# Cast and output buffer counts, the engine that zeroes small operands, and the order of steps in a fused retention and token-mixing kernel

## The chip, the cores and the metric

The kernel runs on one core of a Trainium2 chip. The metric is device time in microseconds (us); 103.92 us is the median of three runs of the kernel before (103.59 to 105.15).

A run is called slow when it is more than 1.5% above the fastest run of the same kernel. A ratio is the mean time of one kernel's fast runs over that of the other's fast runs of the same rounds, so it is not quite the ratio of the medians quoted beside it. Names of engines: PE is the matrix engine, DVE vector, ACT scalar, POOL GpSimd, SP the engine that issues all transfers.

## The reference, cut to what matters

```python
# q, k, v: (B=4, H=8, S=768, D=64) float32
for t in range(S):                               # retention, per head
    state = gamma * state + outer(k[t], v[t])
    y[t]  = q[t] @ state / sqrt(D)
x     = y as (4, 768, 512)
W_tok = scale * (x @ w_q) @ (x @ w_k).T          # token mixing, per batch
out   = relu(W_tok @ x) @ w_out                  # (4, 768, 512) float32
```

## The kernel before

The work is cut into 12 pairs of chunks, three pairs to a batch. Each engine's instructions follow one list of steps, `ORDER`, which an annealer found. A step names the operation, the pair and sometimes the half, then the engine (`:A`, `:V`, `:P` for ACT, DVE, POOL) and the PSUM banks (`@`). The steps that the argument uses:

- `ck`, `cq`, `cv`: cast of k, q, v to bf16 (k and q with the decay factors), into one of `N_CAST` buffers;
- `trk`, `trq`, `xt`: eight transposes on PE; `ekT`, `eqT`, `exN` copy their result out of PSUM;
- `st`: adds k times v to the running state in PSUM; `es` copies the state to SBUF;
- `mx`: mixing matmul, `r` its relu, `pj` the output projection, `eo` copies it to an output buffer and issues the store;
- `warmup`, `fill`: matmuls on zeros that compute nothing; they were put in to keep PE busy, in the hope of a higher granted clock.

```python
N_CAST, ... , N_OUT = 4, ... , 6
...
bank7_ps = psum.tile([128, 512], FP32, name="bank7_ps")
fill_ps  = bank7_ps[:, 256:512]          # the fills write here
state_ps = bank7_ps[:, 0:256]...         # the running state lives here
...
for part in LOADS:                       # k0 q0 v0 k1 q1 k2 q2 v1 v2 W K1 WO Q1 V1
    ... nc.sync.dma_start(...)           # every load and store: SP, one queue
...
def cast(e, name, p, table):
    t = buf(name + "s", p % N_CAST, [2, H, D], BF16)
    ...
    elif casts[name, b] == NP and b + 2 < B:
        load(name, b + 2)                # loads of batches 2 and 3, after the casts of b
...
def fill(e, at, n):
    for _ in range(n):
        nc.tensor.matmul(out=fill_ps, lhsT=warm[:, 0:128], rhs=warm[:, 0:256],
                         start=False, stop=False, skip_group_check=True)
...
def es(e, at, p, c):                     # evicts the state of bank 7
    ... DVE: one tensor_tensor with a mask; ACT: two copies ...
...
def eo(e, at, p, j):
    o = buf(f"o{j}_", p % N_OUT, [DM], FP32)
    copy(e, o, st["o_ps", j])
    nc.sync.dma_start(out=dst[:, j], in_=o)
```

In the program as built, a copy into a used output buffer waits until the store of its previous content has landed (7.25 us in e4, 8.14 in e9).

## Time and profile before

| | before |
|---|---|
| time, median | 103.92 us |
| span of the profile | 103.6 us |
| PE / DVE / ACT / POOL busy | 87% / 64% / 57% / 57% |
| moved, at a mean of | 26.69 MB, 258 GB/s |
| first mixing matmul | 32.07 us |
| last load issued / first store issued / first store landed | 58.76 / 61.84 / 71.1 us |
| last copy of an output | 99.69 us |

Read it as three parts. Until 32 us (the head) PE depends on casts, copies and loads and is partly idle. From there to about 75 us PE is nearly full while the transfers still stream. After that PE sets the pace and the remaining stores go out. A loss in the middle or the end is taken to come out at the end directly, since PE has little slack there: it is busy for 38.45 of 41.06 us from 32.07 to 73.13 us, and for 26.31 of 26.56 us from there to 99.69. The lines themselves stand in the prediction.

### The profile page before, as it was taken

What the parts mean: (1) busy time and instruction counts of PE and PEld (TensorE: products, weight loads), DVE (VectorE), ACT (ScalarE), POOL (GpSimd) and SP (SyncE); (2) the same over time, 40 slices, a digit from 0 to 9 for tenths busy, and PEclk for the clock granted to TensorE, in tenths of its full rate; (3) what the DMA queues carried; (4) which work ended last, traced back from release to release, by engine and by line L of the source; (5) the groups of instructions that cost most, each with busy time, mean ns of one, the idle gap of its engine ahead of it and who ended that gap; (6) DMA issues with size and microseconds to landing.
All of it is one profiled execution on the core that took longest, in us unless ns stands there. A gap on an engine that the chain in (4) does not pass through costs nothing.

```text
span 103.6 us, 3459 instructions
## 1 busy us (share of the span) xinstructions
PE 90.2 (87%) x1477; PEld 61.3 (59%) x1485; DVE 66.6 (64%) x90; ACT 59.5 (57%) x106; POOL 58.7 (57%) x73
## 2 busy tenths in 40 slices
PE   5997876875996999897998999999999999999940
PEld 2345554664884645565895575889666589533410
DVE  3043699754534636989587885796996875625630
ACT  6004508642735665564779777787489796655420
POOL 6999914807953999096699997599930000000000
PEclk9999999999589999999999999999999999999999
DMA  0999998998999999598989999979954220046572
GB/s 23 314 347 346 348 350 220 304 303 321 358 331 301 297 252 334 135 334 278 328 243 308 276 345 357 340 247 364 398 213 164 101 101 6 0 158 247 202 296 112
DMA packets 26079, 26.69 MB, mean 258 GB/s; under 512 B 1744, under 2 KB 20176, under 8 KB 26064
## 3 DMA queue, kind: packets, MB, share of 16 engines
q1 hardware_dynamic: 26064, 26.48, 79.1%
q8 instruction: 11, 0.18, 0.7%
q14 instruction: 4, 0.03, 0.1%
HBM read 20.19 MB, written 6.29 MB: 255 GB/s over the span
## 4 chain that ended last, share of the span: by engine, by line
PE 66%; DVE 13%; POOL 8%; ACT 6%; issue 3%; DVEq 0%; POOLq 0%; ACTq 0%
PE bank_ps L704 17%; PE bank_ps L394 9%; DVE at L462 6%; PE bank_ps L600 5%; PE duo_ps L439 4%; DVE at L455 3%; PE bank_ps L551 3%; PE bank_ps L683 3%; PE bank_ps L624 3%; PE bank_ps L657 3%; PE duo_ps L704 3%; POOL ks L356 2%; PE bank_ps L506 2%; PE bank_ps L634 2%; PE bank_ps L535 2%
## 5 line engine op out<-in xcount | busy, mean ns | idle before, releaser
L462 DVE TENSOR_TENSOR at<-duo_ps,cmask 128x1024 bf16<-128x1024 f32 x18 | 21.4, 1216 | 2.2 <-PE duo_ps L439 2.2
L362 POOL TENSOR_TENSOR ks<-k_st,fk 128x512 bf16<-128x512 f32 x18 | 18.8, 1076 | 5.5 <-PE bank_ps L551 5.5
L704 PE MATMUL bank_ps<-wout_sb,relu 128*128 128x512 bf16 x78 | 19.7, 380 | 0.4 <-issue 0.2
L362 POOL TENSOR_TENSOR qs<-q_st,fq 128x512 bf16<-128x512 f32 x16 | 16.3, 1050 | 6.2 <-DMA q_st<-in_q_dram 6.2
L704 PEld LDWEIGHTS <-relu 128*128 128x128 bf16 x96 | 8.5, 98 | 9.0 <-issue 0.8
L156 ACT COPY o<-bank_ps 128x512 f32<-128x512 f32 x15 | 8.7, 590 | 7.3 <-PE bank_ps L704 7.3
L158 POOL CAST vs<-v_st 128x1024 bf16<-128x1024 f32 x10 | 10.5, 1073 | 4.2 <-DMA v_st<-in_v_dram 4.1
L156 ACT CAST s_sb<-bank_ps 128x256 bf16<-128x256 f32 (+1 forms) x20 | 7.4, 372 | 6.6 <-PE bank_ps L551 4.5
L156 ACT COPY qT<-bank_ps 128x1024 bf16<-128x1024 bf16 x7 | 7.1, 1015 | 5.4 <-PE bank_ps L394 5.4
L696 ACT ACTIVATE relu<-bank_ps 128x512 bf16<-128x512 f32 x15 | 8.5, 599 | 2.5 <-PE bank_ps L683 2.5
L156 ACT CAST xT<-bank_ps 128x512 bf16<-128x512 f32 x12 | 7.0, 590 | 3.6 <-PE bank_ps L524 1.4
L455 DVE TENSOR_TENSOR at<-duo_ps,cmask 128x1024 bf16<-128x1024 f32 x6 | 7.3, 1220 | 2.2 <-PE duo_ps L428 1.6
L329 PE MATMUL bank_ps<-warm 128*128 128x512 bf16 x24 | 7.3, 477 | 1.2 <-DVE warm L227 1.2
L394 PE MATMUL bank_ps<-identity,qs 128*128 128x128 bf16 x88 | 6.8, 220 | 1.4 <-DVE kT L158 0.7
L551 PE MATMUL bank_ps<-vs,ks 128*64 128x64 bf16 (+1 forms) x200 | 6.8, 197 | 1.0 <-ACT s_sb L156 0.9
L394 PEld LDWEIGHTS <-qs 128*128 128x128 bf16 x96 | 5.8, 98 | 3.1 <-issue 1.1
L158 DVE COPY x<-bank_ps 128x1024 bf16<-128x1024 bf16 x7 | 4.8, 688 | 4.3 <-PE bank_ps L600 4.3
L439 PE MATMUL duo_ps<-qT,kT 64*128 64x128 bf16 x144 | 6.6, 217 | 0.9 <-DVE qT L158 0.5
L394 PEld LDWEIGHTS <-ks 128*128 128x128 bf16 x96 | 5.7, 97 | 2.4 <-issue 0.9
L600 PE MATMUL bank_ps<-identity,xT 128*128 128x128 bf16 x88 | 6.7, 225 | 0.0
L551 PEld LDWEIGHTS <-ks 128*64 128x64 bf16 (+1 forms) x200 | 5.0, 110 | 2.8 <-issue 1.1
L158 DVE CAST xT<-bank_ps 128x512 bf16<-128x512 f32 x7 | 4.7, 688 | 2.9 <-PE bank_ps L524 1.3
(96 smaller groups left out, 166.0 us busy)
## 6 DMA issues: line engine op xcount, KB each, us to landing
out_dram<-o SPq DMA_DIRECT2D x24, 256.0 KB, 2.5
k_st<-in_k_dram SPq DMA_DIRECT2D x3, 512.0 KB, 6.0
q_st<-in_q_dram SPq DMA_DIRECT2D x3, 512.0 KB, 6.0
v_st<-in_v_dram SPq DMA_DIRECT2D x3, 512.0 KB, 6.2
wout_stage<-in_moe_w_out_dram SPq DMA_DIRECT2D x1, 1024.0 KB, 10.9
wq_stage<-in_moe_w_q_dram SPq DMA_DIRECT2D x1, 128.0 KB, 6.4
wk_stage<-in_moe_w_k_dram SPq DMA_DIRECT2D x1, 128.0 KB, 5.2
k_st<-in_k_dram SPq DMA_DIRECT2D x3, 0.2 KB, 12.2
```

What stands on the lines that cost most here:

```text
L156: nc.scalar.copy(out=out, in_=in_)
L158: ENGINES[e].tensor_copy(out=out, in_=in_)
L329: nc.tensor.matmul(out=bank(6), lhsT=warm[:, 0:128], rhs=warm, start=True, stop=True)
L362: ENGINES[e].tensor_tensor(out=t[:, j].rearrange("p (o m) d -> p o m d", o=2), in0=in_[:, j].rearrange("p (m o) d -> p o m d", o=2), in1=t ...
L394: nc.tensor.transpose(ps[:, i, hp, :] if whole(name, p // NP) else slots[:, :, hp, i, :], pairs[p][name + "s"][:, i, 2 * hp : 2 * hp + 2, ...
L439: nc.tensor.matmul(out=ps[:, x, m, :], lhsT=st["kT"][rows(x), i, m, :], rhs=st["qT"][rows(x), i, m, :], start=(m == 0), stop=(m == HP - 1) ...
L455: nc.vector.tensor_tensor(out=t.rearrange("p x (hi j) t -> p (x hi) (j t)", j=2), in0=ps.rearrange("p x (hi j) t -> p (x hi) (j t)", j=2), ...
L462: nc.vector.tensor_tensor(out=t.rearrange("p x hp t -> p (x hp) t"), in0=ps.rearrange("p x hp t -> p (x hp) t"), in1=cmask.rearrange("p o ...
L551: nc.tensor.matmul(out=state_ps[rows(x), m, :], lhsT=st["ks"][ps, slot, 2 * m + x, :], rhs=st["vs"][ps, slot, head(p, m, x), :], start=(n ...
L600: nc.tensor.transpose(ps[:, c, a, :], xT(p, a, c), identity)
L696: nc.scalar.activation(out=dst, in_=st["mx"][half], func=ACT.Relu)
L704: nc.tensor.matmul(out=ps, lhsT=st["relu", a // 2][:, a % 2, j], rhs=wout_sb[:, a, :], start=(a == 0), stop=(a == NDM - 1),)
```

## The change

Four edits: six cast buffers instead of four for each of q, k and v; four output buffers for each half instead of six, which pays for them in memory; the zeroing of the small operands on vector instead of GpSimd, which was late with its first cast; and a newly annealed order, with 28 warm-ups instead of 24 and 41 fills instead of 5. The order's diff replaces the whole list.

```diff
-warmup.24 cv.0:A cq.0:V trq.0@4 ck.0:P trk.0@5 eqT.0:V fill.1
+warmup.28 ck.0:V trk.0@4 ekT.0:A cq.0:V fill.6 trq.0@5 eqT.0:V
+fill.6 sc.0.0@0+1 cv.0:P eat.0.0:V sc.0.1@2+3 st.0.0 es.0.0:A fill.6
+st.0.1 ck.1:P in.0.1@4 ia.0.0@5 eat.0.1:V ia.0.1 trk.1@6 ex.0.0:V
+ck.2:V es.0.1:V ex.0.1:A ekT.1:A cq.1:P fill.3 trq.1@4 xt.0@5
 ... (cut)
-pj.5.1@4 ... pj.5.0@2 ... eo.5.1:A eo.5.0:A          (pair 5 fifth)
+r.5.1:A r.5.0:A pj.4.1@4 eo.4.1:A trq.8@2 eat.7.1:V in.7.0@5+6 in.7.1
+ia.7.0 st.7.1 xt.6@4 eqT.8:A ...                      (pair 4, half 1, fifth)
 ... (cut)
-N_CAST, ..., N_OUT = 4, 3, 6, 4, 3, 6, 8, 2, 6
+N_CAST, ..., N_OUT = 6, 3, 6, 4, 3, 6, 8, 2, 4
 ...
-        nc.gpsimd.memset(t, 0.0)          # four state buffers; dmask likewise
+        nc.vector.memset(t, 0.0)
```

More of the change, by code (lines that the diff above doesn't have):

```diff
@@ L18 @@
 ORDER = """
-warmup.24 cv.0:A cq.0:V trq.0@4 ck.0:P trk.0@5 eqT.0:V fill.1
-st.0.0 ekT.0:V fill.1 sc.0.0@0+1 eat.0.0:V es.0.0:A st.0.1 es.0.1:A
-ck.1:P in.0.1@4 sc.0.1@2+3 eat.0.1:V trk.1@5 ekT.1:V ck.2:V cq.1:P
-ia.0.0@6 fill.2 trq.1@5 ia.0.1 eqT.1:A trk.2@2 in.1.0@5 sc.1.1@0+1
-ex.0.1:A cv.1:P ekT.2:A ex.0.0:V cq.2:V trq.2@4 eat.1.1:V sc.1.0@2+3
-st.1.0 eat.1.0:V cv.2:P W:P eqT.2:A sc.2.1@0+1 xt.0@4 es.1.0:A
-in.1.1@6 ia.1.0 ia.1.1 st.1.1 es.1.1:V exN.0:V wqk.0@2 ex.1.1:A
-eat.2.1:V ex.1.0:A in.2.0@4 st.2.0 es.2.0:A sc.2.0@0+1 eat.2.0:V xt.1@5
@@ L27 @@
-exN.1:A ew.0:A in.2.1@6 ia.2.0 ia.2.1 wqk.1@5 ex.2.1:V ex.2.0:A
-wqk.2@4 xt.2@6 exN.2:V ew.2:A ew.1:A fill.1 za.0@4 zm.0
-ez.0:A mx.0@4+5 r.0.1:A ck.3:P ck.4:P ck.5:P cq.3:P cq.4:P
-cq.5:P cv.3:P cv.4:P cv.5:P WO:V mx.1@6+2 r.0.0:A r.1.1:A
-trk.3@5 trk.4@4 ekT.3:A ekT.4:V pj.0.0@2 trk.5@4 r.1.0:A pj.0.1@5
-eo.0.1:A eo.0.0:V ekT.5:V mx.2@6+2 pj.1.1@4 r.2.0:V pj.1.0@5 eo.1.1:A
-trq.3@4 r.2.1:A pj.2.1@6 eo.2.1:A eqT.3:V eo.1.0:A sc.3.0@0+1 eat.3.0:V
-trq.4@4 sc.3.1@2+3 pj.2.0@5 eat.3.1:V eqT.4:A sc.4.0@0+1 eat.4.0:V eo.2.0:A
@@ L35 @@
-sc.4.1@2+3 trq.5@4 st.3.0 es.3.0:V ia.3.0@5+6 ia.3.1 in.3.1 st.3.1
-eqT.5:A eat.4.1:V es.3.1:A sc.5.1@0+1 st.4.0 es.4.0:V ex.3.1:A sc.5.0@2+3
-eat.5.1:V eat.5.0:V in.4.0@4+6 ia.4.0 in.4.1 ia.4.1 st.4.1 es.4.1:A
-st.5.0 ex.4.1:V ex.4.0:A ex.3.0:V es.5.0:A in.5.0@4+2 ia.5.1 in.5.1
-ia.5.0 ex.5.0:A ex.5.1:A xt.4@6 exN.4:V xt.3@5 wqk.3@4 exN.3:A
-ew.3:A xt.5@6 wqk.4@2 wqk.5@4 ew.4:A ck.7:P ck.6:P trk.6@5
-trk.7@2 exN.5:V cq.6:V ew.5:A zm.1@4 ekT.6:A trq.6@6 ekT.7:A
-ez.1:V mx.3@4+5 r.3.1:A cq.7:P eqT.6:V sc.6.0@0+1 eat.6.0:V r.3.0:A
@@ L43 @@
-sc.6.1@2+3 trq.7@5 pj.3.1@4 eqT.7:A pj.3.0@6 eo.3.1:A mx.5@4+5 sc.7.0@0+1
-ck.8:P eat.6.1:V eo.3.0:A r.5.1:A trk.8@2 cv.6:P st.6.0 ia.6.0@6+5
-ia.6.1 eat.7.0:V sc.7.1@0+1 r.5.0:A es.6.0:A in.6.1 st.6.1 cq.8:P
-pj.5.1@4 ex.6.1:A es.6.1:A ex.6.0:A ekT.8:V trq.8@5 pj.5.0@2 eat.7.1:V
-cv.7:P cv.8:P eqT.8:V mx.4@5+6 sc.8.1@0+1 st.7.0 eo.5.1:A eo.5.0:A
-in.7.0@4+2 ia.7.0 es.7.0:A ia.7.1 r.4.1:A r.4.0:V st.7.1 es.7.1:A
-eat.8.1:V wqk.6@5 in.7.1 sc.8.0@0+1 st.8.0 ew.6:A ck.9:P xt.6@5
-trk.9@6 es.8.0:A ex.7.0:V ex.7.1:V wqk.7@4 exN.6:A in.8.0@2+5 in.8.1
@@ L51 @@
-eat.8.0:V ia.8.1 ia.8.0 ekT.9:A ck.10:P cq.9:P ew.7:V trk.10@4
-xt.7@6 ex.8.1:V ex.8.0:A xt.8@5 trq.9@2 ekT.10:A exN.7:V eqT.9:V
-exN.8:V wqk.8@4 ew.8:A sc.9.1@0+1 eat.9.1:V sc.9.0@2+3 cq.10:P trq.10@6
-eat.9.0:V pj.4.0@4 pj.4.1@5 eqT.10:A sc.10.0@0+1 eo.4.0:V cv.9:A eo.4.1:A
-zm.2@6 st.9.0 ez.2:A es.9.0:A ia.9.0@4+2 ia.9.1 mx.6@5+6 eat.10.0:V
-in.9.1 r.6.0:A st.9.1 sc.10.1@0+1 r.6.1:V cq.11:P ck.11:P cv.10:P
-cv.11:P trq.11@5 trk.11@6 ex.9.1:V es.9.1:A ex.9.0:A pj.6.0@4 ekT.11:V
-eqT.11:A pj.6.1@5 eat.10.1:V st.10.0 eo.6.0:A sc.11.1@2+3 eo.6.1:A sc.11.0@0+1
@@ L59 @@
-mx.7@4+6 es.10.0:A wqk.9@5 st.10.1 r.7.0:A eat.11.1:V r.7.1:A es.10.1:A
-in.10.0@4+2 in.10.1 ia.10.0 ia.10.1 st.11.0 ew.9:A eat.11.0:V in.11.0@5+6
-ia.11.1 ia.11.0 es.11.0:V in.11.1 ex.11.1:V ex.10.0:A ex.10.1:A xt.9@4
-xt.10@2 ex.11.0:A xt.11@5 exN.11:V exN.10:V exN.9:A wqk.11@6 ew.11:V
-wqk.10@4 ew.10:A pj.7.1@5 eo.7.1:A mx.8@4+6 za.3@2 zm.3 r.8.1:V
-r.8.0:A pj.7.0@5 ez.3:A pj.8.1@4 mx.9@6+2 eo.7.0:A eo.8.1:V pj.8.0@5
-r.9.1:A r.9.0:A mx.10@4+2 eo.8.0:A r.10.0:V pj.9.0@6 eo.9.0:V pj.9.1@4
-eo.9.1:V r.10.1:A mx.11@5+6 pj.10.0@2 eo.10.0:V pj.10.1@4 eo.10.1:V r.11.0:A
@@ L67 @@
-r.11.1:A pj.11.1@5 eo.11.1:V pj.11.0@6 eo.11.0:A
+warmup.28 ck.0:V trk.0@4 ekT.0:A cq.0:V fill.6 trq.0@5 eqT.0:V
+fill.6 sc.0.0@0+1 cv.0:P eat.0.0:V sc.0.1@2+3 st.0.0 es.0.0:A fill.6
+st.0.1 ck.1:P in.0.1@4 ia.0.0@5 eat.0.1:V ia.0.1 trk.1@6 ex.0.0:V
+ck.2:V es.0.1:V ex.0.1:A ekT.1:A cq.1:P fill.3 trq.1@4 xt.0@5
+eqT.1:A trk.2@6 sc.1.0@0+1 cq.2:V fill.5 trq.2@4 sc.1.1@2+3 exN.0:A
+eat.1.0:V ekT.2:A eqT.2:A cv.1:P fill.3 st.1.0 sc.2.0@0+1 eat.1.1:V
+cv.2:P es.1.0:A ck.5:P ck.4:P fill.1 sc.2.1@2+3 st.1.1 in.1.1@4
@@ new lines @@
+es.1.1:V fill.2 st.2.0 eat.2.1:V W:A wqk.0@5 ck.3:P es.2.0:A
+ew.0:A in.1.0@6 in.2.1@2 eat.2.0:V cq.4:P in.2.0@5 ia.2.0 ia.2.1
+ex.2.0:V ex.2.1:A fill.4 xt.2@5 exN.2:V ia.1.0 ia.1.1 wqk.2@2
+ex.1.1:A ew.2:A cq.3:P cq.5:P ex.1.0:V xt.1@4 exN.1:A wqk.1@5
+cv.3:P cv.4:P fill.2 trk.5@6 ew.1:A za.0@4 zm.0 ez.0:A
+ekT.5:V fill.1 mx.0@4+5 r.0.0:A r.0.1:A mx.1@6+2 fill.2 trk.4@4
+cv.5:P WO:V pj.0.1@5 eo.0.1:V r.1.0:A r.1.1:A pj.0.0@6 eo.0.0:V
+mx.2@5+2 ekT.4:A pj.1.0@4 trk.3@6 r.2.0:V pj.1.1@5 r.2.1:A eo.1.0:V
@@ new lines @@
+ekT.3:A eo.1.1:A trq.4@4 eqT.4:V pj.2.0@6 sc.4.0@0+1 sc.4.1@2+3 trq.3@4
+pj.2.1@5 eat.4.0:V eat.4.1:V eo.2.0:A eqT.3:A sc.3.0@0+1 trq.5@4 eat.3.0:V
+eo.2.1:A sc.3.1@2+3 st.3.0 ia.3.0@5+6 es.3.0:V st.3.1 eqT.5:A sc.5.0@0+1
+in.3.1 es.3.1:A st.4.0 eat.3.1:V in.4.0@4+2 ia.3.1 es.4.0:A ex.3.1:A
+ex.3.0:A st.4.1 eat.5.0:V in.4.1 es.4.1:V sc.5.1@0+1 st.5.0 es.5.0:A
+ia.4.0 ia.4.1 eat.5.1:V ex.4.0:A in.5.0@5+6 in.5.1 ia.5.1 ia.5.0
+ex.5.0:A ex.5.1:V wqk.5@4 xt.3@5 xt.5@6 ex.4.1:V ew.5:V xt.4@4
+wqk.3@2 exN.3:A wqk.4@5 exN.5:V ck.7:P ck.6:P ew.3:A trk.6@6
@@ new lines @@
+trk.7@2 ew.4:A exN.4:V zm.1@4 cq.6:V ekT.6:A ez.1:V trq.6@5
+mx.3@4+6 ekT.7:A eqT.6:V cq.7:P trq.7@2 r.3.1:A eqT.7:A sc.6.0@0+1
+mx.4@5+6 r.3.0:V pj.3.0@4 sc.6.1@2+3 eat.6.0:V eat.6.1:V sc.7.0@0+1 r.4.1:A
+eo.3.0:A ck.8:P cv.6:P trk.8@6 st.6.0 r.4.0:A ekT.8:V ia.6.0@4+5
+ia.6.1 es.6.0:A st.6.1 es.6.1:A in.6.1 ex.6.1:A ex.6.0:A pj.3.1@6
+mx.5@5+2 eat.7.0:V sc.7.1@0+1 cv.7:P st.7.0 es.7.0:V eo.3.1:V cq.8:P
+r.5.1:A r.5.0:A pj.4.1@4 eo.4.1:A trq.8@2 eat.7.1:V in.7.0@5+6 in.7.1
+ia.7.0 st.7.1 xt.6@4 eqT.8:A cv.8:P wqk.6@2 es.7.1:V st.8.0
@@ new lines @@
+ia.7.1 sc.8.0@0+1 ew.6:A exN.6:V sc.8.1@2+3 pj.5.0@4 ex.7.1:A es.8.0:A
+ex.7.0:V wqk.7@5 eo.5.0:A eat.8.1:V ew.7:A xt.7@6 exN.7:A in.8.0@4+2
+in.8.1 ia.8.1 eat.8.0:V ia.8.0 ex.8.1:V ck.9:P ck.10:P trk.10@5
+trk.9@6 cq.9:P ex.8.0:A xt.8@4 ekT.10:A ekT.9:V trq.9@2 wqk.8@5
+eqT.9:V sc.9.0@0+1 eat.9.0:V sc.9.1@2+3 cq.10:P ew.8:A exN.8:A trq.10@5
+eqT.10:V pj.4.0@6 pj.5.1@4 sc.10.1@0+1 cv.9:A st.9.0 eo.5.1:A eo.4.0:A
+eat.9.1:V zm.2@5 es.9.0:V ez.2:A eat.10.1:V ia.9.0@4+2 ia.9.1 in.9.1
+ex.9.0:A st.9.1 mx.6@5+6 cq.11:P cv.11:P r.6.1:A r.6.0:A ck.11:P
@@ new lines @@
+sc.10.0@0+1 trq.11@4 trk.11@6 pj.6.0@5 cv.10:P es.9.1:V eat.10.0:V st.10.0
+eqT.11:A ekT.11:V mx.7@4+6 ex.9.1:A sc.11.1@0+1 sc.11.0@2+3 es.10.0:A st.10.1
+eo.6.0:V r.7.1:A es.10.1:A r.7.0:A in.10.0@5+6 in.10.1 ia.10.0 ia.10.1
+st.11.0 ex.10.1:A pj.6.1@4 eat.11.0:V eo.6.1:A ex.10.0:V wqk.10@5 xt.10@6
+xt.9@4 eat.11.1:V ew.10:A in.11.0@5+2 es.11.0:A in.11.1 ia.11.0 ia.11.1
+ex.11.0:A exN.9:A exN.10:V ex.11.1:V pj.7.0@6 eo.7.0:V xt.11@5 wqk.9@2
+wqk.11@4 exN.11:V ew.9:V mx.8@5+6 za.3@2 ew.11:A zm.3 pj.7.1@4
@@ L68 @@
+r.8.0:A r.8.1:A ez.3:V mx.9@5+6 r.9.1:V eo.7.1:A r.9.0:A pj.8.0@2
+eo.8.0:V mx.10@4+5 pj.8.1@6 r.10.0:A r.10.1:V eo.8.1:V pj.9.0@2 eo.9.0:A
+pj.9.1@4 mx.11@5+6 r.11.0:A eo.9.1:A pj.10.1@2 eo.10.1:A r.11.1:V pj.11.1@5
+eo.11.1:A pj.11.0@4 eo.11.0:A pj.10.0@5 eo.10.0:A
 """.split()
@@ L74 @@
 LOADS = "k0 q0 v0 k1 q1 k2 q2 v1 v2 W K1 WO Q1 V1".split()
-N_CAST, N_QKT, N_AT, N_S, N_XT, N_X, N_WQK, N_RELU, N_OUT = 4, 3, 6, 4, 3, 6, 8, 2, 6
+N_CAST, N_QKT, N_AT, N_S, N_XT, N_X, N_WQK, N_RELU, N_OUT = 6, 3, 6, 4, 3, 6, 8, 2, 4
 @with_exitstack
@@ L305 @@
     for t in s2_sbs:
-        nc.gpsimd.memset(t, 0.0)
+        nc.vector.memset(t, 0.0)
     dmask = const("dmask", [1, 2, D], BF16)
-    nc.gpsimd.memset(dmask, 0.0)
+    nc.vector.memset(dmask, 0.0)
     for x in range(2):
-        nc.gpsimd.memset(dmask[rows(x), :, x, :], 1.0)
+        nc.vector.memset(dmask[rows(x), :, x, :], 1.0)
     wq_sb = const("wq_sb", [NDM, 2, DH], BF16)
```

## The prediction

> **What bounds the kernel now.** I read the page's slices first, then the chain, then the matrix engine alone, then the transfer queue.
>
> ```profile
> PE   5997876875996999897998999999999999999940
> PEclk9999999999589999999999999999999999999999
> DMA  0999998998999999598989999979954220046572
> ```
>
> The matrix engine (PE) is nearly full from about the twentieth slice (52 us) on; before that it has gaps, and in the eleventh and twelfth (26 to 31 us) its granted clock falls once. The transfers are near full until about 75 us. So two resources are close to their limit: PE, and one stream of transfers.
>
> ```profile
> PE 66%; DVE 13%; POOL 8%; ACT 6%; issue 3%; DVEq 0%; POOLq 0%; ACTq 0%
> 3.00:6.00 3.00, 3.00 (x10) 1.13 (x9) 0.00 (x0) 0.00 (x0) 2.81 (x9) 1.00 1.15 344
> 24.00:27.00 3.00, 2.00 (x36) 1.61 (x39) 1.44 (x2) 1.24 (x3) 3.00 (x4) 0.78 1.01 372
> 27.00:30.00 3.00, 3.00 (x68) 2.83 (x68) 0.69 (x1) 1.41 (x3) 3.00 (x4) 0.65 1.01 365
> 73.13:99.69 26.56, 26.31 (x360) 15.83 (x363) 18.39 (x24) 17.35 (x33) 2.83 (x3) 1.00 0.42 158
> ```
>
> The first line is the chain that ended last: two thirds PE. The others are stretches (length; busy PE, weight load, DVE, ACT, POOL; clock; DMA share; GB/s). From 73 us to the last matmul PE is busy 26.31 of 26.56 us: any time lost before there comes out at the end. In 24 to 30 us the clock costs about 0.22 x 3 + 0.35 x 3 = 1.7 us.
>
> The queue that all transfers use, around the last load and the first output:
>
> ```profile
> 53.56 4.75 SPq L196 DMA_DIRECT2D q_st<-in_q_dram  x1
> 58.76 3.02 SPq L196 DMA_DIRECT2D v_st<-in_v_dram  x1
> 61.84 6.95 SPq L719 DMA_DIRECT2D out_dram<-o  x1
> ...
> DMA to landing us min/median/max: 9.3/9.3/9.3
> ```
>
> This is what I rest on. Every load and store is issued by SyncE, in program order, on one queue; all loads stand before the 24 stores. The first store, whose data had been in its buffer since about 37 us, is issued at 61.84, when the last load (v of batch 3) is out; its issue takes 6.95 us (later ones 0.33) and it lands after 9.3, at 71.14. The loads are not held by buffers: the last one needs the casts of v of batch 1, over at 41.7 us, and is issued at 58.76 only because the stream ahead is full.
>
> [...] in the trace DVE's zeroing of 512 bf16 is run as 256 uint32 and takes 0.27 us, POOL's 0.53.
>
> **The change part by part.**
>
> *Zeroing on vector.* It takes from POOL 1.92 (four state buffers) + 0.21 + 0.33 (mask) = 2.5 us, which stood ahead of POOL's first cast of k at 7.10 us. On DVE it is about 4 x 0.27 + 0.3 = 1.4 us, within DVE's wait of 4.41 us for q. Free.
>
> *New order at the head.* The first k cast goes to DVE. q landed at 6.5 and v at 7.94, so k should land near 5.1, and k is cast at 6.3. But there are 28 warm-up matmuls for 24; the 24 held PE until 8.4[...]. Then transpose k (0.45), six fills (0.65), transpose q (0.45), its copy (0.69 after a latency of 0.16): the first scores start at about 11.7, against 10.96. There are 41 fills for 5: 36 x 0.108 = 3.9 us of PE, mostly where it waited. Worked on by hand with the trace's durations (eviction and mask 1.22 on DVE, copy 1.02 on ACT, 0.69 on DVE), batch 0's first mixing matmul comes at about 32.7 instead of 32.1, with one more transpose (0.45) done and no fall of the clock. Up to 44 us I find the two level within 0.7 us.
>
> *Six cast buffers.* POOL's waits of 5.5 us for buffers are mostly waits for a load anyway (k of batch 1 goes into an unused buffer at 23.95 and still waits). The loads do not start earlier, for the reason above. Worth near 0.
>
> *Four output buffers, with the new order.* Buffer numbers are the pair modulo four, so pair 4 now writes into pair 0's buffers; with six, pair 6 was the first to reuse. In the new order ACT's copy of pair 4's second half stands after the two relus of pair 5 and before the q copy of pair 8, and the build shows that it waits for a transfer: the first store. When does ACT get there? PE, from batch 1's last z product to that projection, has by the steps' issue times (8 transposes 0.45, 8 scores 0.33, projection 4 x 0.217 = 0.87, state 0.24, the rest likewise) 8.6 us. In the kernel before that z product starts at 54.26; with its kind of gaps (0.7) the projection ends at about 63.5. The first store lands at 71.14, since the stream of loads is not touched. ACT stands for 7.5 us. PE has five small groups left (trq.8, in.7.0, in.7.1, ia.7.0, st.7.1: 0.45 + 0.46 + 0.27 + 0.24 = 1.4 us), then needs the bank that the waiting copy has to empty: it stands from about 65.0 to 71.14 + 0.1 + 0.59 = 71.85.
>
> From there all the rest is PE work. Counted from the order: 12 groups of transposes x 0.45 = 5.4; 8 scores x 0.33 = 2.6; 6 states x 0.24 = 1.4; 7 x 0.23 and 9 x 0.27 for y = 4.0; 6 projections of q and k x 0.67 = 4.0; 2 z x 0.78 = 1.6; 6 mixes x 0.33 = 2.0; 15 output projections x 0.87 = 13.1. Sum 34.1 us. The same count for the kernel before from 73.13 gives 26.4, where the trace has 26.56, so the count can be trusted. [...] Small waits 0.8. PE ends at 71.85 + 34.1 + 2.2 + 0.8 = 108.95. The end after the last matmul (copy, store, landing) is 103.6 - 99.7 = 3.9. Span 112.9; the kernel before has 103.92 on the clock for a span of 103.6, so some 0.3 more, and the annealer may have left fewer waits than I put in: 112.8.
>
> **The rivals.**
>
> 1. *The head and the fills win.* PE's idle time from its first transpose to its end is some 8 us and the fallen clock 1.7; a better order could take 2 to 4 of it: 100 to 102 us. For it: the fills stand where PE waited, and the fall goes. Against: whatever the head wins ends at the wait for the first store, whose time is set by 20 MB of loads and not by compute. Only if that wait is not there does it count.
>
> 2. *The stream ends earlier.* Bandwidth dips to 135 GB/s in one slice; if the new rhythm closed the dips, the first store would land earlier. The queue's instructions are the same in the same order, the casts that free the staging buffers are over more than ten microseconds before, so I give it 1 us at most: 111.5.
>
> 3. *Nothing moves.* If the store did not queue behind the load (landing 2.5 us after 61.84, 64.3), ACT would wait under 1 us and the result would be 102 to 104.5. The trace shows 9.3 us for just this store, so this is unlikely.
>
> 4. *Longer penalty.* [...] the order, tuned for other times, makes more waits: 115 to 116.
>
> **Range and chances.** Rival 3 with 1 gives about one chance in twelve for less than 106. Otherwise the landing is known within 1 us, the count within 1, the clock's loss within 1.5: 109.5 to 115.5, middle 112.8. Faster by over 2%: 0.04; within 2%: 0.05; slower by over 2%: 0.91.
>
> **What would show it.** Right: a wait of ACT for the store of o of 6 us or more near 64 to 71 us, the longest in the list of waits; PE empty in the slices around 65 to 71 us; granted clock near half just after; the first store issued near 62 and landed near 71; more than 34 us from that landing to the last matmul; POOL without zeroing. The fall of the clock at 26 to 30 us gone. Wrong: ACT's copy of pair 4 without a wait, or the first store landing before 66 us; or PE busy through 65 to 71 us; then the head decides and I am wrong by 8 us.

## More of the kernel before

Verdicts use fast runs alone.

In the order before, the sequence of output copies is pairs 0, 1, 2, 3, 5, 4, 6 to 11; the two copies of pair 5 start at 63.13 and 64.41 us.

## The result, and the profile after

The change made the kernel slower. The four runs took 108.58, 114.85, 108.42 and 110.67 us, median 109.62, against 103.85 for the kernel before (four runs). Two of them are fast; fast against fast the ratio is 1.0457 (interval 1.0414 to 1.0499). The prediction was 112.8 with a range of 109.5 to 115.5: the median is just inside, the fast runs are below it. The profiled run is a fast one (108.58), and it does not show what the prediction rests on. That the change came out slower, as forecast, is luck in these fast runs: their loss is another one.

The slices of the kernel after, to be read against those that the prediction opens with:

```profile
PE   5999691996989899989589999999999999999950
PEclk9999999599999999999999999999999999999999
DMA  1999999989999799999999999973005022205593
```

No hole of PE at 65 to 71 us (slices 25 to 27) and no fall of the clock there. The deep hole is in the seventh slice, at 16 to 18.7 us, and the clock is lowest in the eighth: it is at 0.50 from 18.4 to 21.8 us. (The half-empty twentieth slice holds a gap of 1.06 us for which the profile shows no cause.) The milestones place the loss:

| | before | after | difference |
|---|---|---|---|
| first scores | 10.96 | 11.50 | +0.54 |
| first mixing matmul | 32.07 | 35.93 | +3.86 |
| last z product of batch 1 | 54.26 | 58.28 | +4.02 |
| last copy of an output | 99.69 | 103.13 | +3.44 |
| span | 103.6 | 106.9 | +3.3 |

All that the profiled execution lost, it lost between 11.5 and 36 us. From the first mixing matmul on both kernels take the same time (67.6 us before, 67.2 after, to the last copy). The 3.3 us of the profiles are less than the 4.7 us between the fast runs (108.5 against 103.8 on the mean), because the profiled execution of the kernel before took 105.34 us, 1.4 us above the median of its timed runs. The chain of waits of the kernel after (start, length, what; each piece was waited for by the next) shows how:

```profile
12.42 0.36 ACT s_sb L157
12.80 0.38 ACT s_sb L157
13.21 0.81 PE bank_ps L334 x6
...
15.38 0.57 issue
15.95 1.61 DVE ks L357
17.56 0.61 DVE s_sb L570
18.21 0.67 PE bank_ps L334 x3
18.89 0.85 PE bank_ps L395 x8
```

`L334` is the fill. Three fills, which compute nothing, wait for DVE's eviction of the state (`s_sb`, step `es.0.1`), and that eviction stands behind DVE's cast of k of pair 2 (`ks`, 1.61 us). Behind the fills come transposes that had nothing to wait for, and they run at 0.85 us for eight where the same eight take 0.45 at full clock. PE's list of waits says how much of the waiting is before fills (total, times, longest):

```profile
PE bank_ps L334 <- DVE s_sb L570: 2.9, 2, 2.4
PE bank_ps L334 <- ACT s_sb L157: 1.3, 2, 0.8
```

That is 4.2 us at four places. All fills write into the half of bank 7 beside the running state, and the state's eviction reads the other half; in the program as built a fill after an `st` waits for that `es`. In stretches (length; busy PE, weight load, DVE, ACT, POOL; clock; share and rate of transfers):

```profile
15.00:18.00 3.00, 0.85 (x32) 0.64 (x21) 2.66 (x3) 1.52 (x2) 1.24 (x2) 1.00 1.12 304
18.00:21.00 3.00, 2.79 (x25) 2.66 (x25) 1.91 (x2) 1.23 (x2) 0.84 (x1) 0.56 1.08 327
21.00:24.00 3.00, 3.00 (x67) 2.20 (x66) 1.76 (x2) 2.52 (x3) 0.62 (x1) 0.87 0.89 240
```

PE works 0.85 of 3 us, then the clock is at 0.56 and 0.87: about 0.44 x 3 + 0.13 x 3 = 1.7 us of PE's work lost. The fall of the kernel before (1.7 us by the same sum; 0.50 from 25.7 to 29.1 us) has not gone, it has moved. Ahead of the fall in the kernel before, PE's longest gap between 22.0 and 25.3 us was 0.70 us, and PE was busy for 1.55 of these 3.30 us; ahead of that in the kernel after the longest gap was 2.36 us. What makes the clock fall is not shown by this. Nor is that fall in every execution of the kernel before: of its 19 fast runs beside the experiments, nine have a mean granted clock of 1.0 (103.73 to 104.62 us) and nine one of 0.983 or 0.984 (104.53 to 105.47 us), as the profiled one has.

And the store? Its queue on SP, then the copy that had to wait for it, on ACT:

```profile
49.80 5.15 SPq L197 DMA_DIRECT2D q_st<-in_q_dram  x1
55.42 3.26 SPq L197 DMA_DIRECT2D v_st<-in_v_dram  x1
58.73 14.20 SPq L720 DMA_DIRECT2D out_dram<-o  x10
...
DMA to landing us min/median/max: 8.8/8.8/8.8
```

```profile
66.48 0.59 ACT L697 ACTIVATE relu<-bank_ps 128x512 bf16<-128x512 f32 x1
67.57 0.58 ACT L157 COPY o<-bank_ps 128x512 f32<-128x512 f32 x1 [0.49 <-DMA out_dram<-o]
```

(The line of 8.8 us is for the first store alone.) The wait that the prediction put at 7.5 us is there, on the very instruction named, and lasts 0.49 us. The head was late, so ACT came to this copy at 67.1 instead of about 63.6; and the stream was early, so the first store was issued at 58.73 and landed at 67.5 instead of 71.1. A microsecond of the stream's gain can be seen where the kernel before had a hole, before first, after second:

```profile
42.00:43.00 1.00, 0.74 (x16) 0.42 (x16) 1.00 (x2) 0.64 (x2) 0.00 (x0) 1.00 0.23 50
```

```profile
42.00:43.00 1.00, 1.00 (x13) 0.64 (x10) 0.45 (x1) 0.74 (x2) 1.00 (x2) 1.00 1.04 352
```

50 GB/s against 352 (last column); what gave the rest of the 3.6 us was not found. So there were two theories to test. The store theory (S where an expectation uses letters): four output buffers cost a wait of many microseconds for the first store, which the fast runs of the kernel after do not show only because their head is late and their stream early; mend the head, and the wait comes out. Its rival, the fill theory: the fills in the state's bank are what is wrong with this kernel, and the buffers cost next to nothing, as the profile's 0.49 us says; mend the head, and the time falls by as much.

### The profile page after: what moved, and what is told of

Read it like the earlier page. It is cut to its first block, busy times and chain, and to the rows that moved or that the text cites. A ratio compares the mean times of both kernels' runs of the same rounds, so it can differ in the third digit from the quotient of the medians.

```text
span 106.9 us, 3535 instructions
## 1 busy us (share of the span) xinstructions
PE 93.3 (87%) x1515; PEld 64.5 (60%) x1525; DVE 70.3 (66%) x99; ACT 61.9 (58%) x105; POOL 54.4 (51%) x64
## 4 chain that ended last, share of the span: by engine, by line
PE 76%; DVE 11%; issue 5%; ACT 5%; DVEq 0%; ACTq 0%
PE bank_ps L705 16%; PE bank_ps L395 8%; PE bank_ps L330 7%; PE bank_ps L601 6%; DVE at L463 6%; PE bank_ps L334 4%; PE bank_ps L552 4%; PE bank_ps L684 3%; PE duo_ps L440 3%; PE bank_ps L536 3%; PE duo_ps L705 3%; PE bank_ps L625 2%; PE bank_ps L507 2%; PE bank_ps L658 2%; ACT s_sb L157 2%
## 5 line engine op out<-in xcount | busy, mean ns | idle before, releaser
L363 POOL TENSOR_TENSOR qs<-q_st,fq 128x512 bf16<-128x512 f32 x16 | 17.2, 1108 | 2.9 <-DMA q_st<-in_q_dram 2.8
L159 POOL CAST vs<-v_st 128x1024 bf16<-128x1024 f32 x11 | 11.2, 1037 | 8.6 <-DMA v_st<-in_v_dram 8.6
L157 ACT COPY kT<-bank_ps 128x1024 bf16<-128x1024 bf16 x7 | 7.1, 1020 | 7.8 <-PE bank_ps L395 7.7
L334 PE MATMUL bank_ps<-warm 128*128 128x256 bf16 x41 | 6.7, 279 | 4.2 <-DVE s_sb L570 2.9
L330 PE MATMUL bank_ps<-warm 128*128 128x512 bf16 x28 | 7.9, 453 | 1.3 <-DVE warm L228 1.3
L157 ACT CAST s_sb<-bank_ps 128x256 bf16<-128x256 f32 (+1 forms) x15 | 5.6, 371 | 5.5 <-PE bank_ps L552 5.1
L157 ACT COPY qT<-bank_ps 128x1024 bf16<-128x1024 bf16 x5 | 5.1, 1014 | 4.4 <-PE bank_ps L395 4.4
L395 PE MATMUL bank_ps<-identity,ks 128*128 128x128 bf16 x88 | 7.0, 228 | 0.1
L157 ACT COPY x<-bank_ps 128x1024 bf16<-128x1024 bf16 x6 | 6.1, 1015 | 1.7 <-PE bank_ps L601 1.7
L159 DVE CAST xT<-bank_ps 128x512 bf16<-128x512 f32 x6 | 4.1, 688 | 4.1 <-PE bank_ps L536 2.2
```

The costliest lines, as they stand in the source:

```text
L157: nc.scalar.copy(out=out, in_=in_)
L159: ENGINES[e].tensor_copy(out=out, in_=in_)
L330: nc.tensor.matmul(out=bank(6), lhsT=warm[:, 0:128], rhs=warm, start=True, stop=True)
L363: ENGINES[e].tensor_tensor(out=t[:, j].rearrange("p (o m) d -> p o m d", o=2), in0=in_[:, j].rearrange("p (m o) d -> p o m d", o=2), in1=t ...
L395: nc.tensor.transpose(ps[:, i, hp, :] if whole(name, p // NP) else slots[:, :, hp, i, :], pairs[p][name + "s"][:, i, 2 * hp : 2 * hp + 2, ...
```

## The experiments

Twelve runs were made, in three calls; those of a call share one chip and the runs of the kernel before (103.73 to 105.94 us with e1 to e4, 103.96 to 105.93 with e5 to e8, 103.73 to 106.89 with e9 to e12). The profiles of e1, e5, e6 and e8 are of slow runs.

### e1: the eviction ahead of the cast

```diff
-ck.2:V es.0.1:V ex.0.1:A ekT.1:A cq.1:P fill.3 trq.1@4 xt.0@5
+es.0.1:V ck.2:V ex.0.1:A ekT.1:A cq.1:P fill.3 trq.1@4 xt.0@5
```

> The changed kernel with two neighbouring DVE steps of the head exchanged: the eviction of the state (es.0.1) before the cast of k of pair 2 (ck.2), so that the three fills that wait for that eviction start at about 15.7 instead of 18.2 us. Theory F (the head is lost to fills that wait for state evictions of the same PSUM bank, and to the fall of the clock that follows): batch 0's first mixing matmul (before 32.1, changed kernel 35.9) comes at 32 to 33.5. Theory S (four output buffers: ACT's copy of pair 4 waits for the first store, which lands at 67.5 in the changed kernel): then ACT comes to that copy at 63.5 to 65 and waits 2.5 to 4 us, so the end gains little: 106.5 to 108.5 us. If S is wrong the gain of the head reaches the end: 104 to 105.5. If F is wrong nothing moves: mixing at 35 to 36, 108 to 109.

Measured: correct, 115.09, 112.53, 114.86, 113.15; ratio 1.0822 (1.0719 to 1.0925). The longest wait of a fill fell to 0.83 us and the first mixing matmul came at 34.3 instead of 35.93: the direction that the fill theory gives, but less than the expected 32 to 33.5. The end got worse, not better: in the profile (of a slow run) the first store was issued at 62.86 and landed at 71.6, and ACT waited 5.9 us for it. The expected end was a miss, because I had taken the early landing of 67.5 as a property of the kernel.

### e2 and e3: the old buffer counts in the new order

```diff
-N_CAST, ..., N_OUT = 6, ..., 4
+N_CAST, ..., N_OUT = 4, ..., 6      # e2 with the swap of e1, e3 without
```

> The same exchange, and the buffers as in the kernel before (four for casts, six for outputs). Under S the wait of ACT for the first store is gone, because pair 6 is the first to reuse an output buffer; under F the head is as in the run before. Both together: 103 to 105 us, and the difference from the run with four output buffers is what S is worth: 2.5 to 4 us. If S is wrong the two runs are equal within 0.5 us. A rival (six cast buffers are worth something in this order) would make this run slower than its partner.

> The changed kernel with the buffers as before (four for casts, six for outputs), nothing else undone. In its own trace ACT waits 0.49 us for the first store. Under F with S hidden behind the late head: 108 to 108.6 us, at most 0.5 us less than the changed kernel. If the prediction's mechanism (the store) were the cause of the loss, this run would be back at 104 to 105.

Measured: e2 110.81, 110.84, 112.64, 111.01 (ratio 1.0635), e3 110.71, 110.44, 109.57, 109.68 (ratio 1.0559), and both results wrong (relative error of e2 1.2e11), which was not intended. The new order casts pair 5's k before pair 1's state has read its own; with four buffers these are one and the same buffer. (This is read off the order; no run tests it alone.) POOL's k casts also waited 11.0 us in e3 for buffers to be released, and its first mixing matmul came at 38.0 us. So these say nothing of the store. The new order needs more than four cast buffers: with four it is neither right nor on time.

### e4: no fills

```diff
-warmup.28 ck.0:V trk.0@4 ekT.0:A cq.0:V fill.6 trq.0@5 eqT.0:V
+warmup.28 ck.0:V trk.0@4 ekT.0:A cq.0:V trq.0@5 eqT.0:V
 ... (all 12 groups of fills, 41 matmuls, taken out)
```

> The changed kernel without any of its 41 fill matmuls (warm-up of 28 kept). Under F the waits of 0.8, 2.4, 0.5 and 0.5 us of PE for state evictions through fills vanish and 41 x 0.108 = 4.4 us of PE work too; the head's transposes come 1 to 3 us sooner[...]. Mixing of batch 0 at 32 to 34.5. With S behind it the end gains 0 to 2 us only: 106.5 to 108.5; ACT's wait for the first store is over 1.5 us. If fills are not to blame: mixing at 35 to 36.

Measured: correct, 112.7, 112.3, 112.98, 112.37; ratio 1.0794 (1.0714 to 1.0875). Without its 41 useless matmuls the kernel is slower than the fast runs of the kernel after (1.0794 against 1.0457); but the kernel after was not run in this call, and its slow runs are as long (e5). The first mixing matmul came at 32.4, 3.5 us earlier than in the kernel after, and then ACT and PE in this profile:

```profile
69.84 0.58 ACT L156 COPY o<-bank_ps 128x512 f32<-128x512 f32 x1 [7.25 <-DMA out_dram<-o]
```

```profile
70.48 1.01 PE L600 MATMUL bank_ps<-identity,xT 128*128 128x128 bf16 x8 [6.32 <-ACT o L156]
```

```profile
64.00:70.50 6.50, 0.18 (x11) 0.17 (x6) 0.60 (x2) 0.66 (x2) 5.86 (x6) 0.86 0.99 334
70.50:74.00 3.50, 3.50 (x46) 2.91 (x47) 1.15 (x2) 1.67 (x3) 3.50 (x5) 0.50 1.01 383
```

PE works 0.18 of 6.5 us, and the 3.5 us after that run at half clock. (Before the wait the clock was at 1.00; it fell while PE stood.) This is the store theory's wait in a fast run, with ACT's 7.25 us where the prediction had 7.5, PE's 6.32 where it had 6.8. The copy ends at 70.4 and PE's last matmul at 107.2: 36.8 us, where the prediction summed 34.1 + 2.2 + 0.8 = 37.1 (the 2.2 us, for the clock after the wait, were my estimate, not shown by a trace). My expected end of the run was again a miss by some 5 us, for the reason of e1.

### e5 to e8: the kernel after again, and a pool of ten output buffers

e5 is the kernel after, unaltered. e6 lets all outputs take one pool of ten buffers in turn, so that no output made before the first store lands needs an old one; the six cast buffers stay. e7 is e6 without the four groups of fills that waited (12 of 41 matmuls). e8 is e6 without fills.

```diff
-    for i in range(N_OUT):
-        for j in range(2):
-            buf(f"o{j}_", i, [DM], FP32)
+    for i in range(10):
+        buf("o", i, [DM], FP32)
+    turn = [0]
...
-        o = buf(f"o{j}_", p % N_OUT, [DM], FP32)
+        o = buf("o", turn[0] % 10, [DM], FP32)
+        turn[0] += 1
```

```diff
 # e7 besides (e8: as e4 besides)
-fill.6 sc.0.0@0+1 cv.0:P eat.0.0:V sc.0.1@2+3 st.0.0 es.0.0:A fill.6
+fill.6 sc.0.0@0+1 cv.0:P eat.0.0:V sc.0.1@2+3 st.0.0 es.0.0:A
-ck.2:V es.0.1:V ex.0.1:A ekT.1:A cq.1:P fill.3 trq.1@4 xt.0@5
+ck.2:V es.0.1:V ex.0.1:A ekT.1:A cq.1:P trq.1@4 xt.0@5
 ... (fill.1 ahead of sc.2.1 and fill.2 behind es.1.1 taken out likewise)
```

> The changed kernel once more, unaltered, to see how its executions scatter. Theory S+F (two causes that hide each other: with a late head ACT meets the first store as it lands, with an early stream of loads nothing is lost there, with a late one up to 5 us are): its runs scatter much more than the kernel before (103.7 to 105.9 so far): 107.5 to 115, the slower ones with a lower granted clock (0.95 to 0.96 for 0.984), because PE then stands in the middle and the clock falls a second time. A theory of the head alone: all runs within 1.5 us of 108.5.

> The changed kernel, its output buffers arranged as one pool of ten, taken in turn (2 more in all than four and four; the eleventh output is the first to reuse one), all else unaltered, six cast buffers. S says: no wait of ACT for a store, and so no scatter: 107.5 to 108.8 in every fast run, no run over 110. F says that the head's loss stays: first mixing at 35.5 to 36.5. The prediction's mechanism as the whole cause would give 104 to 105.

> The pool of ten and the four fill groups taken out that wait for a state eviction (12 of 41 fills); 29 fills stay. F: the wait of 2.4 us and two of the smaller ones go, the clock does not fall before 30 us; first mixing at 31.5 to 33.5; with S out of the way the gain reaches the end: 103 to 105 us. If the head were not paid in full at the end: over 106.

> The pool of ten and no fills. The run without fills but with four output buffers had its first mixing at 32.4 and ACT waiting 7.3 us for the first store, 112.5 us. S: that wait and the second fall of the clock go, 6 to 9 us less: 103.5 to 106. If the wait were not the cause of those 112.5 us, this run stays above 110.

| | runs | fast against fast, over the kernel before | first mixing matmul | store landed, ACT's wait for it |
|---|---|---|---|---|
| e5, after again | 115.68, 112.6, 111.7, 109.77, 116.2, 113.72 | none given (one fast run) | 35.2 | 73.2, 7.4 |
| e6, ten buffers | 108.66, 108.33, 106.81, 108.67 | 1.0284 (1.018 to 1.0389) | 36.0 | 68.1, none |
| e7, and 12 fills less | 106.15, 105.94, 105.51, 105.35 | 1.0109 (1.005 to 1.0169) | 32.3 | 69.6, none |
| e8, and no fills | 104.63, 102.97, 106.27, 102.58, 103.99, 103.32 | 0.9826 (0.9747 to 0.9905) | 32.7 | 69.3, none |

All correct. Three readings follow.

First, e8 against e4. The two differ in the output buffers alone; four fast runs of each have 112.3 to 112.98 and 102.58 to 103.99 us. Against the kernel before they stand at 1.0794 and 0.9826, some 9.7% of its time apart. That is the cost of the output buffers, measured with the head on time.

Second, e6, e7 and e8 among themselves. With the store's wait out of the way, the 12 waiting fills cost 107.6 - 105.7 = 1.8 us of the means of the fast runs, and all 41 cost 107.6 - 103.2 = 4.4 us (e6 has only two fast runs, 1.5 us apart). e6 still shows the fill's wait of 2.2 us behind DVE's eviction, e7 none. So the fill theory has the cause of the head's loss right, and is wrong in that the buffers cost nothing. No run keeps these fills and moves them to another bank or place. e7 missed the expected 103 to 105 us, since a part of the gain went again at the end: the last copy is at 99.39 us, but the last stores took 2.7 to 4.0 us to land, where 2.0 to 3.1 are usual.

Third, e5 against e6. The kernel after spreads from 109.77 to 116.2 us, wider than the expected 107.5 to 115; with ten output buffers nothing is above 108.7. The profile of e5, of its slow run of 115.68, has the store landing at 73.2 and ACT waiting 7.4 us. So the same program waited 0.49 us in one execution and 7.4 in another. One profile of a slow run does not prove that all of the slower runs are of this kind; that they vanish with the buffers speaks for it, but two of the five slow runs (112.6 and 111.7 us) have no lower clock than the fast one (0.985 and 0.979 for 0.977), where a lower one was expected. So this third reading is not shown.

### e9 and e10: single parts of the change in the kernel before

```diff
 # e9
-N_CAST, ..., N_OUT = 4, ..., 6
+N_CAST, ..., N_OUT = 6, ..., 4
 # e10
-nc.gpsimd.memset(...)      # three places
+nc.vector.memset(...)
```

> The kernel before with six cast buffers and four output buffers, its order unaltered. Its own order writes pair 4's outputs only at 75 us and later, after the first store has landed (71.1), so S says that four output buffers cost nothing here, and six cast buffers bring nothing, as the loads are paced by their own stream: equal to the kernel before within 0.6 us. If the buffers alone were the fault: slower by 2 us or more.

> The kernel before with the zeroing of the small operands moved to vector, nothing else. POOL's first cast of k starts at about 5 instead of 7.1 us (k has landed), so PE's second transposes start right after the first, at 8.8 to 9.0 instead of 9.55, and the first scores 0.5 to 0.7 us sooner. At the end 0 to 0.7 us less than the kernel before: 103.3 to 105 on a chip where that has 104 to 105.

Measured for e9: correct, 114.95, 115.04, 113.82 fast and 115.77; ratio 1.0985 (1.0854 to 1.1115; the record's verdict is unclear, though the whole interval lies above 2%). I had expected no change, and that was plainly wrong: I had looked at pair 4, which the old order projects at about 75 us, and overlooked that pair 5 comes at about 63 and, modulo four, takes pair 1's buffers. Its profile, the copy on ACT first, then lines of the list of waits and the slices of the clock:

```profile
70.34 0.59 ACT L156 COPY o<-bank_ps 128x512 f32<-128x512 f32 x1 [8.14 <-DMA out_dram<-o]
```

```profile
ACT o L156 <- DMA out_dram<-o: 9.0, 2, 8.1
PE bank_ps L506 <- ACT o L156: 6.8, 1, 6.8
PE duo_ps L506 <- ACT o L156: 1.1, 1, 1.1
```

```profile
PEclk9999999999999999999999995556999999999998
```

Here the buffer counts alone cost 10% in an order made for six output buffers. The clock falls for four slices, from 68 to 79 us, around the end of PE's wait of 6.8 us. The six cast buffers changed with them, but the head shows no loss (first mixing matmul at 31.0 us), and the waits are for output stores. This is the cleanest test of the store theory, and it uses nothing of the new order.

Measured for e10: correct, 105.76, 106.22, 105.21, 106.33, all fast; ratio 1.0148 (1.0051 to 1.0246), verdict unclear. The zeroing itself took DVE 1.09 + 0.11 + 0.28 = 1.48 us in its idle time, and POOL's first k cast started at 5.07 instead of 7.10 us, as meant. Nothing was gained: the second group of transposes started at 9.41 instead of 9.55, since in this execution the 24 warm-ups ran until 8.97 instead of 8.38. In the old order that cast was not what the head waited for longest.

### e11 and e12: 24 warm-ups

```diff
-warmup.28 ck.0:V trk.0@4 ...      # in e8 (giving e11) and in e7 (giving e12)
+warmup.24 ck.0:V trk.0@4 ...
```

> The changed order, pool of ten output buffers, no fills, and 24 warm-ups as before for 28. The run with 28 had its first transpose at 9.7 us and 102.6 to 104 us. [...] first transpose at 8.5 to 9.0, first mixing at 31.5 to 32, 102 to 103.3 us. If the head is absorbed later (the loads pace it): as before within 0.4 us.

> The same with 29 fills (the four groups that wait for a state eviction stay out) and 24 warm-ups. Its partner with 28 had no fall of the clock, first mixing at 32.3, but 105.4 to 106.2 us because its last stores took 2.7 to 4.0 us to land for 2.0 to 2.5. If that was a property of the executions: 102.5 to 104. If it is a property of the program it comes again: 104.5 to 106.

Measured for e11: correct, 103.16, 102.8, 103.24, 104.3, ratio 0.9915 (0.9784 to 1.0046); first transpose at 9.24 us (8.5 to 9.0 expected if the four warm-ups counted in full, 9.67 in e8) and first mixing matmul at 31.6 instead of e8's 32.7, with no gain in time that is clear of the noise. For e12: correct, 105.17, 107.2, 105.78, 105.25, ratio 1.0103 (1.0 to 1.0205); first mixing matmul at 32.9 instead of e7's 32.3, so no gain, and with e7's late end again (last copy at 99.05, span 103.5). What delays the last stores in e7 and e12 stays open.

e8 is the best version that ran: by the ratios it beats the kernel after by about 6% and the one before by 1.7%, with the verdict unclear. e11 is of the same rank (medians of 103.66 and 103.2 on two chips).

## Why the prediction was right or wrong

**Right: the mechanism and its size, where the head is on time.** The store stands behind all loads, ACT stops in order at the first copy into a used buffer, PE stops when it needs the bank that this copy empties, and the clock halves. e4 (fast runs) shows each link with 7.25, 6.32 and 0.50 where the prediction had 7.5, 6.8 and a clock near half, and 36.8 us of PE to the end where it had 37.1. e9 shows it with nothing but the buffer counts changed: 10%.

**Right: the zeroing, and the head up to the first scores.** DVE did the zeroing in 1.48 us (1.4 predicted) before its first cast at 4.90 us; the warm-ups ended at 9.17 and the first scores started at 11.50 (11.7). (A warm-up took 0.216 us in the trace, 3.24 us for 15.) That POOL's late first cast was worth mending, e10 does not show.

**Wrong: "mostly where it waited" and "Up to 44 us I find the two level within 0.7 us."** This is the first step that failed. The first mixing matmul came at 35.93 and not at 32.7. I had counted the fills as 3.9 us of PE's time put into holes, and looked at no dependency of their own. They share bank 7 with the state, so four groups waited 4.2 us for evictions of it, and useful transposes waited behind them. The clock fell after the longest of these waits (2.36 us), to a mean of 0.56 over 18 to 21 us, in the place where the fills were meant to hold it up. That fills hold it up was my assumption, not shown: the mean granted clock of the fast runs was 0.988 to 0.995 with the other 29 fills (e7) and 0.978 to 1.0 with none (e8). e6 to e7 shows what these four groups cost, 1.8 us between fast runs.

**Wrong: "otherwise the landing is known within 1 us."** This is the second. It landed at 67.5 and not 71.14 in the profiled run. The prediction's second rival, a stream that ends earlier, came true, with its size put at 1 us at most; it was 3.6, of which the closed dip shows about one. So PE was busy through 65 to 71 us, which the prediction had named as a sign that it was wrong. Over the fourteen profiles it landed between 67.5 and 74.1 us, and for one and the same program at 67.5 and (in a slow run) at 73.2. One profile cannot tell such a landing within 1 us.

The two misses have opposite signs for ACT, which came 3.5 us later and met a store that was 3.6 us earlier: 7.5 - 7.1 leaves about 0.4, and 0.49 was measured. That is why a fast run of the kernel after shows almost nothing of the fault that costs 10% alone, and why e1 and e4, which repaired the head, were slower than its fast runs.

**Wrong in part: six cast buffers "Worth near 0".** The new order does not work with four (e2 and e3). Whether they also move the stream is open: e9's first store landed at 69.0 and e10's, with four cast buffers, at 70.4, but single profiles of one program differ by more.

**A small one.** I added 0.3 us from span to time, by setting the span of one run against the median of others. Each run has 1.7. It made the prediction 1.4 us too low and thereby looks better than its terms.

**What stays open.** What makes the stream of loads end at different times, and whether every slow run of the kernel after is a late store, were not settled. Only three of its ten runs are fast, and the median of all ten is 112.15 us, near the predicted 112.8; whether these runs pay what the prediction describes is known for the one slow run that was profiled (e5).

## What to carry to other kernels

When stores share a queue with loads and stand behind them, count the outputs that are made before the last load is through: the output buffers should cover all of them. The first store took 8.8 to 9.3 us from issue to landing in the profiles of before, after, e4 and e9, against a median of 2.2 to 2.6 for all their stores. Too few buffers cost PE 6.3 us of waiting in e4 and 6.8 in e9, and work at a granted clock of 0.50 after that (70.5 to 74 us in both). Whether a second queue for the stores would avoid it was not tried. Fillers that wrote into a bank under eviction waited like real work (2.4 us at the longest) and held real work up; a bank of their own was not tried. Two faults can hide each other, so test each one with the other taken away, and read more than one execution before calling a transfer's landing known.
